# The opening of a fused recurrence and two expert layers: first maxima from the first chunk's own gates, and products that nobody reads

## The chip, the cores and the metric

The kernel runs on one core of a Trainium2 chip. A time is the device time of one execution in microseconds (us). The core has a matrix engine (TensorE, PE in the rows; its weight loads are PEld), a vector engine (DVE), a scalar engine (ACT), GpSimd (POOL) and the sync engine (SP), which here issues nearly all transfers between HBM and SBUF. Each engine takes its instructions strictly in the order written; between engines, semaphores hold an instruction until what it needs is there. Products land in PSUM, eight banks of 128 partitions x 512 floats.

## The reference, cut to what matters

Three layers follow one another: a gated linear recurrence over 768 steps (2 batches x 8 heads, head size 40), a gated MLP on the 1536 tokens (320 -> 1536 -> 320), and a mixture of 8 experts with the best two taken (320 -> 1024 -> 320). Everything is in float32. The change lies in the recurrence:

```python
m_new = max(f_t + m, i_t)              # running maximum, per batch and head
f_stab, i_stab = exp(f_t + m - m_new), exp(i_t - m_new)
C = f_stab * C + i_stab * outer(v_t, k_t)
n = f_stab * n + i_stab * k_t
y_t = sigmoid(o_t) * (C @ q_t) / max(|n @ q_t|, 1)
```

## The kernel before

The 768 steps are cut into 6 chunks of 128. A chunk of one batch (`ci` = 0 to 11; chunk `ci // 2`, batch `ci % 2`) is computed as attention inside the chunk plus a state `st[b]` carried from chunk to chunk. Let F be the sum of the forget gates since the chunk's start, a = i - F, and cm the running maximum of a. Then the weight of step s for step t is exp(a_s - Ml_t), where Ml = max(cm, what comes in from the chunks before). `g0` makes F, a and cm for all 96 (batch, head, chunk) rows (L418 to L420, 96 partitions x 128), `g1` and `g2` carry the maxima from chunk to chunk and make Ml (L429 to L439), which is also written to DRAM (`ml_d`), from where the later chunks read it spread over 128 partitions (`load_mb`, L378). The first two `ci` do not wait for that round trip: `gb` (L446, step `m`) spreads eight rows of Ml over 128 partitions by float32 products with a column of the identity matrix repeated 128 times, four heads to a PSUM bank of the tag `acc`, of which there are two.

The work of one `ci`, by the letters of the step table: `e` exponentials of the weights (ACT, four per half of the heads, L482); `s` products q.k (L500); `p` their multiplication with the weights (DVE L505) and the mask (POOL L506); `v` products with v (L557); `u` products k.v for the state (L518), `d` and `S` the state's decay and sum (L531, L539), `c`/`C` the state's part of the result (L526, L549); `y`, `z` division and gate (DVE L563 to L576); `t` transposes (L356); `X`, `x` the split of the result into two parts whose sum has float32 precision (ACT L340, DVE L343); `k` weighted keys (L490); `o` tanh of the output gate (L591).

The MLP's weight tiles go through a decode and split (`D` for the first, `N` for the second matrix, parts `r`, `a`, `b`, `c`, `h`/`H`, `l`; DVE L260, L263, L266, L298, L299, ACT L257, POOL L273). A unit of the MLP is `G` and `V` (eight products of 128x256 each, L363), `T` tanh, `U` the gating (DVE L884, L887), `H` and `L` a split, `J` the second matrix. Tokens of two `ci` make one unit's input.

Up to about 145 us the order is a table of words, `STEPS`, written out by hand; each engine gets its instructions in that order. After it, loops set the order. The words `w<n>g` and `w<n>a` issue n products of 128 weights by 512 columns in bfloat16 on a matrix of ones (`warm`, L734) into a PSUM bank of tag `gv` or `acc`; nothing reads them. `l` words issue loads: `lm`, `lq`, `lt` (maxima, q and k, tokens of a `ci`), `lu`, `ld` (weight tiles). SP issues transfers in that order and waits at each until the buffer is free. The tables of the experts, the routing and the last stage are not touched.

Of the kernel before, what the change touches and what calls it, by code (L numbers as in the profile page):

```python
# [53 lines left out]
o4 lu3 s4 e5.1 U0.2 w4g x3 G1.0 N0c V1.0 N0H lm6 p4.1 p4.0 u4 N0l T1.0 d4 H0.2 J0.0 G1.1 N1a C4 N1r N1b lu4 L0.2 ld2
K5 U1.0 H1.0 v4.0 o5 N1c e5.0 N1h T1.1 v4.1 S4 y4 lq6 lt6 s5 c5 D3a ld3 z4 D3b D3r C5 N1l w5g t4 X4 V1.1 p5.0 L1.0
lm7 U1.1 p5.1 D3c x4 J0.1 J0.2 e6.0 R0 e6.1 G1.2 V1.2 u5 d5 T1.2 U1.2 lq7 D3H H1.1 v5.0 v5.1 S5 D3l G1.3 lu5 y5 z5
N2r D4r s6 L1.1 p6.0 p6.1 V1.3 t5 T1.3 U1.3 N2a c6 K6 C6 X5 x5 J1.0 H1.3 lt7 lm8 lq8 K7 D4a N2b D4b D4c N2c v6.0
e7.0 lu6 L1.3 d6 G2.0 V2.0 T2.0 U2.0 H1.2 L1.2 v6.1 ld4 o6 y6 N2h D4h u6 S6 N2l e7.1 z6 H2.0 J1.1 L2.0 lt8 s7 p7.0
G2.1 V2.1 p7.1 c7 C7 o7 T2.1 U2.1 H2.1 t6 X6 J1.2 J1.3 D4l u7 L2.1 x6 G2.2 d7 v7.0 lm9 e8.0 T2.2 V2.2 U2.2 S7 lq9 R1
H2.2 e8.1 v7.1 s8 y7 z7 k8 G2.3 V2.3 T2.3 L2.2 p8.0 t7 c8 X7 U2.3 H2.3 o8 C8 p8.1 x7 d8 L2.3 J2.0 v8.0 u8 S8 e9.0  # L60
lt9 K9 e9.1 G3.0 V3.0 T3.0 U3.0 H3.0 v8.1 y8 L3.0 z8 G3.1 s9 p9.1 T3.1 p9.0 D5a c9 J2.1 C9 lm10 lq10 lt10 o9 V3.1
U3.1 e10.0 t8 D5b D5r X8 d9 D5c lm11 D5H G3.2 T3.2 J2.2 J2.3 x8 u9 v9.0 V3.2 H3.1 L3.1 D5l o10 U3.2 S9 v9.1 e10.1 y9
H3.2 z9 R2 lq11 s10 G3.3 p10.0 p10.1 J3.0 t9 V3.3 X9 N3r x9 T3.3 lu7 lt11 e11.0 U3.3 L3.2 H3.3 N3a c10 C10 G4.0 L3.3
# [1206 lines left out]
```

## Time and profile before

| | us |
|---|---|
| runs shown | 556.64, 552.83, 554.41 (median 554.41) |
| the profiled execution, first to last instruction | 551.0 |
| PE busy (weight loads) | 527.7 (506.0) |
| DVE, ACT, POOL busy | 342.6, 251.8, 202.4 |
| transfers | 73.14 MB, mean 133 GB/s |

The profiled execution has no whole time of its own in the page, only its span of 551.0 us; the median of the three runs is 3.4 us longer, and the runs differ by 3.8 us among themselves. A busy PE is not a PE at its peak: a product's end is modelled, and one that is stretched by a slow clock or by its weight load counts as busy all the same. PEclk is the clock that was granted, as a share of 2.4 GHz: 1.00 is 2.4 GHz and 0.50 is 1.2 GHz. Where the trace has no record of the clock yet, at the start of a kernel, the views print 1.00; what the clock was there is read from how long a product takes.

### The profile page before, as it was taken

To read this page: it belongs to the slowest core of one execution; us is meant where nothing else is said; L and a number is where in the kernel's file an instruction comes from. 1 tells how busy PE (TensorE), PEld (TensorE's weight loads), DVE (VectorE), ACT (ScalarE), POOL (GpSimd) and SP (SyncE) were. 2 spreads that over 40 slices of the span, in tenths; PEclk is the share of its full clock that TensorE was granted. 3 is DMA by queue.
4 is the path that set the end of the run, shared out by engine and by line. 5 is a ranking of instruction groups with operands and counts; after the bars stand their busy time and mean duration, and the time that the engine had idled before them with its cause. 6 is when DMAs were issued, how large, how long until landed. Compare 5 with 4: busy or idle time off the path is not lost.

```text
span 551.0 us, 10447 instructions
## 1 busy us (share of the span) xinstructions
PE 527.7 (96%) x3847; PEld 506.0 (92%) x3847; DVE 342.6 (62%) x914; ACT 251.8 (46%) x566; POOL 202.4 (37%) x375
## 2 busy tenths in 40 slices
PE   6999999999999999999999999799999999999993
PEld 4987999998999899999999999699999999999992
DVE  5469999798639988345448853982738283734420
ACT  3426555544345534355445733653646363543420
POOL 6323463332232332226556165214142414242322
PEclk9569999999999999999999999899999999999997
DMA  7839967441474644001112317564645464441403
GB/s 259 233 91 266 334 199 235 127 156 49 127 194 159 213 157 140 25 1 50 48 50 71 112 52 222 171 202 67 223 88 202 86 203 88 162 87 49 64 5 41
DMA packets 39908, 73.14 MB, mean 133 GB/s; under 512 B 3399, under 2 KB 25799, under 8 KB 39847
## 3 DMA queue, kind: packets, MB, share of 16 engines
q1 hardware_dynamic: 34807, 64.10, 36.1%
...
q14 instruction: 29, 0.24, 0.1%
...
## 4 chain that ended last, share of the span: by engine, by line
PE 79%; DVE 13%; ACT 2%; issue 2%; POOL 2%; DMA 1%; SPq 0%; POOLq 0%; ACTq 0%; DVEq 0%
PE gv L363 28%; PE acc L363 8%; PE ps_misc L557 3%; PE gv L1118 3%; PE gv L1119 3%; PE gv L1120 3%; PE acc L796 3%; PE acc L794 3%; PE acc L795 3%; PE ps_s L500 2%; PE ps_s L356 2%; PE acc L1120 2%; PE acc L1119 2%; PE acc L1118 2%; PE acc L1114 2%
## 5 line engine op out<-in xcount | busy, mean ns | idle before, releaser
L363 PE MATMUL gv<-x,wa 128*128 128x256 f32 (+3 forms) x1440 | 212.3, 295 | 4.9 <-ACT x L857 2.4
L363 PEld LDWEIGHTS gv<-x,wa 128*128 128x128 f32 x1440 | 194.8, 190 | 8.3 <-DVE ew L887 3.2
L893 POOL TENSOR_TENSOR h<-ew,h 128x256 fp32r<-128x256 f32 x72 | 57.2, 799 | 101.2 <-ACT h L890 66.4
L1136 POOL DMA_INDIRECT out_dram<-R,idi x33 | 49.5, 1501 | 61.4 <-ACT R L1131 43.3
L363 PE MATMUL acc<-x,wa 128*128 128x416 f32 (+2 forms) x288 | 58.3, 341 | 0.0
L884 DVE SCALAR_TENSOR_TENSOR ew<-ew,gv 128x256 f32<-128x256 f32 x72 | 30.0, 416 | 43.8 <-ACT ew L876 37.9
L876 ACT ACTIVATE ew<-gv 128x256 f32<-128x256 f32 x72 | 27.4, 382 | 63.6 <-PE gv L363 59.9
L332 DVE TENSOR_TENSOR wb<-draw,wb 128x640 fp32r<-128x640 f32 x32 | 27.6, 869 | 45.6 <-ACT wb L329 45.1
L1083 POOL CAST at<-at 128x32 fp32r<-128x32 f32 x72 | 21.5, 313 | 87.9 <-DVE at L1080 71.7
L890 ACT ACTIVATE h<-ew 128x256 fp32r<-128x256 f32 x72 | 29.8, 415 | 45.3 <-DVE ew L887 45.3
L363 PEld LDWEIGHTS acc<-x,wa 128*128 128x128 f32 x288 | 50.0, 189 | 0.4
L794 PE MATMUL acc<-wb,h 128*128 128x320 f32 x144 | 45.9, 320 | 0.0
L795 PE MATMUL acc<-wb,h 128*128 128x320 f32 x144 | 44.3, 309 | 0.0
L796 PE MATMUL acc<-wb,h 128*128 128x320 f32 x144 | 42.6, 313 | 0.4 <-POOL h L893 0.4
L1118 PE MATMUL gv<-wb,at 128*128 128x320 f32 x120 | 37.8, 315 | 0.0
L1120 PE MATMUL gv<-wb,at 128*128 128x320 f32 x120 | 37.2, 310 | 0.4 <-DVE at L1080 0.4
L1119 PE MATMUL gv<-wb,at 128*128 128x320 f32 x120 | 37.1, 309 | 0.0
L307 ACT ACTIVATE wa<-uraw 128x768 fp32r<-128x768 f32 x32 | 26.9, 840 | 12.9 <-DMA uraw<-in_w_dram 11.2
L506 POOL TENSOR_SCALAR_AFFINE_SELECT at<-at 128x512 f32<-128x512 f32 x24 | 17.4, 739 | 38.0 <-DVE at L505 28.8
L887 DVE SCALAR_TENSOR_TENSOR ew<-ew,gv 128x256 f32<-128x256 f32 x72 | 30.1, 417 | 1.7
L329 ACT ACTIVATE wb<-draw 128x640 fp32r<-128x640 f32 x32 | 23.2, 734 | 15.5 <-DMA draw<-in_w_dram 14.0
L298 DVE TENSOR_TENSOR wa<-uraw,wa 128x512 fp32r<-128x512 f32 x32 | 22.5, 703 | 9.7 <-ACT wa L307 9.4
...
## 6 DMA issues: line engine op xcount, KB each, us to landing
uraw<-in_w_dram SPq DMA_DIRECT2D x16, 768.0 KB, 4.8
...
uraw<-in_wup_dram SPq DMA_DIRECT2D x12, 768.0 KB, 9.0
...
```

The costliest lines, as they stand in the source:

```text
L363: m = PE.matmul(ps, w[:, k, ws], x[hl][:, t], start=n == 0, stop=n == len(seq) - 1)
L794: PE.matmul(o, hb[:, 0, os], w_[:, 0, q], start=j == 0, stop=False)
L795: PE.matmul(o, hb[:, 0, os], w_[:, 1, q], start=False, stop=False)
L796: PE.matmul(o, hb[:, 1, os], w_[:, 0, q], start=False, stop=j == len(tiles) - 1)
L884: m = V.scalar_tensor_tensor(t, t, 1.0, gv[:, 0], op0=OP.add, op1=OP.mult)
L887: V.scalar_tensor_tensor(t, t, 0.5, gv[:, 1], op0=OP.mult, op1=OP.mult)
L890: last["hi"] = A.activation(self.hb[:, 0], self.t, AF.Copy)
L893: P.tensor_tensor(self.hb[:, 1], self.t, self.hb.bitcast(F32)[:, 0], op=OP.subtract)
L1118: PE.matmul(acc[:m], h0, w[:, 0, f % 2], start=f == 0, stop=False)
L1119: PE.matmul(acc[:m], h0, w[:, 1, f % 2], start=False, stop=False)
L1120: PE.matmul(acc[:m], h1, w[:, 0, f % 2], start=False, stop=f == EJ - 1)
L1136: s = P.indirect_dma_start(out=out, out_offset=bass.IndirectOffsetOnAxis(ap=ID[v][:m, j:j + 1], axis=0), in_=y, in_offset=None, compute_op ...
```

## The change

Five things are changed together.

1. A new input `first` (80 x 2 x 128, 82 KB) holds the gates of chunk 0 three times, on partitions 0 to 15, 32 to 47 and 64 to 79. `i0` and `i1` make F, a and cm of chunk 0 alone from it, before `g0`. For chunk 0 nothing comes in from before, so its Ml is its cm.
2. cm is cut into three bfloat16 pieces whose sum is cm, one on each of the three partition groups, and `gb` spreads a row by one bfloat16 product with a 0/1 matrix `sel` that adds the three pieces (80 rows, 128 columns).
3. The `w` words of the opening are new in number, place and PSUM tag (`m` is `ps_misc`, `s` is `ps_s`), and one `w4g` further on is gone.
4. The state update is one `scalar_tensor_tensor` per pair of heads, four in all, in place of a multiplication and an addition on all four pairs; the words `d` are gone.
5. The first steps stand in another order, and so do the first transfers: both `ci`'s q, k and tokens come before the two weight tiles, and the two decodes of the weights stand later.

```diff
-g0 o0 w9g D0a D0b s0.02 g1 g2 lm2 lq2 s0.1357 D0r o1 m0.0 e0.0 D0c D0H s0.46 m1.0 e1.0 s1 ld0 p0.0 p1.0 la3 lt2 g3
-m0.1 e0.1 D1a m1.1 e1.1 v0.0 p0.1 w1a v1.0 lb3 w3a v0.1 D0l p1.1 v1.1 D1b y0 e2.0 g4 lu2 D1r z0 lm3 y1 z1 t0 X0 s2
-x0 D1c D1H t1 w4a X1 x1 g5 k0 D1l k1 e2.1 p2.1 p2.0 G0.0 V0.0 G0.1 T0.1 u1 V0.1 lt3 T0.0 u0 S1 U0.0 H0.0 L0.0 D2a S0
+w11g i0 w2g i1 w2g m0.0 m0.1 s0 e0.0 g0 w4g e0.1 m1.0 p0.0 w4g g1 m1.1 w3g g2 p0.1 e1.0 e1.1 s1 p1.0 v0.0 w4s o0 o1 p1.1
+v0.1 y0 D0a D0b w4s v1.0 D0r D0c D0H lm2 lq2 ld0 v1.1 w3s z0 t0 w4s lq3 lt2 X0 g3 x0 y1 z1 t1 w2s D0l X1 x1 g4 lu2 lm3 D1a D1b e2.0 D1r s2 D1c D1H g5 k0
+D1l k1 e2.1 p2.1 p2.0 G0.0 V0.0 G0.1 T0.1 u1 V0.1 lt3 T0.0 u0 S1 U0.0 H0.0 L0.0 D2a S0
...
+    N0 = 80
+    fst = wk.tile([N0, 6, 2, L], F32, name="x", bufs=X_BUFS).rearrange("p a b l -> p (a b) l")
+    SP.dma_start(fst[:, 0:2], first)
+    F0, a0, cm0, r0 = (fst[:, i] for i in range(2, 6))
+    pieces, mid = (fst[:, 6].bitcast(BF)[:, i * L:(i + 1) * L] for i in range(2))
+    sel = fst[:, 7].bitcast(BF)[:, 0:B * H]
...
+    for i in range(0, N0, 32):
+        r = slice(i, min(i + 32, N0))
+        V.tensor_scalar(sel[r], diff[r, i:i + B * H], 0.0, None, op0=OP.is_equal)
...
-    load_qk(0)
-    up_load(0)
-    load_qk(1)
     for ci in range(2):
         MB[ci] = at_tile([128, H, L])
     for ci in range(2):
-        TK[ci] = at_tile([128, 2 * DM + 328])
-    load_tk_in(0)
-    load_tk_in(1)
+        load_qk(ci)
+        load_tk(ci)
+    up_load(0)
     up_load(1)
...
+    def i0():
+        V.tensor_tensor_scan(F0, fst[:, 1], pre[0:N0, 4:4 + L], 0.0, op0=OP.add, op1=OP.add)
+        V.tensor_tensor(a0, fst[:, 0], F0, op=OP.subtract)
+        t = ps_misc()
+        PE.transpose(t[:, 0:N0], a0, ident[:N0, :N0])
+        A.activation(cols[:, 0, :, :, 0], t[:, 0:B * H].rearrange("p (b h) -> p b h", b=B), AF.Copy)
+    def i1():
+        V.tensor_tensor_scan(cm0, a0, a0, -1e30, op0=OP.max, op1=OP.max)
+        V.tensor_copy(pieces, cm0)
+        V.tensor_tensor(r0, cm0, pieces, op=OP.subtract)
+        V.tensor_copy(pieces[32:64], r0[32:64])
+        V.tensor_copy(mid[64:N0], r0[64:N0])
+        V.tensor_tensor(pieces[64:N0], r0[64:N0], mid[64:N0], op=OP.subtract)
...
-            r = (ci * H + 2 * i + half) * NC
-            PE.matmul(m[:, i], ident[:G96, r:r + 1].to_broadcast([G96, 128]), Ml, start=True, stop=True)
+            r = ci * H + 2 * i + half
+            PE.matmul(m[:, i], sel[:, r:r + 1].to_broadcast([N0, 128]), pieces, start=True, stop=True)
...
-        def p_d():
-            if 0 < c < NC - 1:
-                V.tensor_tensor(st[b], st[b], dec2[:, b, :, c:c + 1].to_broadcast([104, 4, 82]), op=OP.mult)
...
-                V.tensor_tensor(st[b], st[b], u, op=OP.add)
+                for q in range(4):
+                    V.scalar_tensor_tensor(st[b][:, q], st[b][:, q], dec2[:, b, q, c:c + 1], u[:, q], op0=OP.mult, op1=OP.add)
...
-            warm(n, {"g": "gv", "a": "acc"}[st_])
+            warm(n, {"g": "gv", "a": "acc", "m": "ps_misc", "s": "ps_s"}[st_])
```

How the instructions stand, at three places. First, TensorE from the first instruction on, before (`ones` is the matrix of the unread products, L734; L446 spreads the maxima; runs of the same product stand once, with "..." for the rest):

```order
L422 MATMUL ps_misc<-shift,x 1x96
L423 MATMUL ps_misc<-shift,x 1x96
L424 MATMUL ps_misc<-ident,x 128x96
L734 LDWEIGHTS ones
L734 MATMUL gv<-ones 128x512
...
L500 MATMUL ps_s<-at 128x128 x2
L433 MATMUL ps_misc<-one_87,rows 96x1
L500 MATMUL ps_s<-at 128x128 x4
L446 MATMUL acc<-x,ident 128x128 x4
```

and the same stretch of the change (L752 is now the unread product, L426 the transpose of `i0`, L467 the spreading, L521 the q.k products, L443 to L445 `g0`):

```order
L752 LDWEIGHTS ones
L752 MATMUL gv<-ones 128x512
...
L426 MATMUL ps_misc<-ident,x 128x80
...
L467 LDWEIGHTS x
L467 MATMUL acc<-x 128x128
...
L521 MATMUL ps_s<-at 128x128 x8
L443 MATMUL ps_misc<-shift,x 1x96
L444 MATMUL ps_misc<-shift,x 1x96
L445 MATMUL ps_misc<-ident,x 128x96
```

Before, TensorE's first instruction needs cm of all 96 rows. Now eleven unread products stand first, then the transpose, four more unread products and the eight spreading products of `ci` 0, and `g0` comes behind the q.k products. In all 43 unread products stand ahead of the first unit of the MLP, where there were 17.

Second, the vector engine around the second token tile's split (the second L343 of the piece before, the second L351 of the one after; L260, L263, L266 or L268, L271, L274 are the decode steps a, b, c of a weight tile, L298 and L299 or L306 and L307 its last step), before:

```order
L343 TENSOR_TENSOR x<-ps_misc,x 128x3x128
L266 ISA dec<-uraw,dec 128x1536
L343 TENSOR_TENSOR x<-ps_misc,x 128x3x128
L459 COPY cols<-acc 128x288
L490 TENSOR_TENSOR kw_112<-at,cols 128x8x40
L298 TENSOR_TENSOR wa<-dec,wa 128x512
L299 TENSOR_TENSOR wa<-dec,wa 64x256
L490 TENSOR_TENSOR kw_113<-at,cols 128x8x40
L505 SCALAR_TENSOR_TENSOR at<-at,ps_s 128x4x128 x2
L884 SCALAR_TENSOR_TENSOR ew<-ew,gv 128x256
```

and in the change:

```order
L306 TENSOR_TENSOR wa<-dec,wa 128x512
L307 TENSOR_TENSOR wa<-dec,wa 64x256
L351 TENSOR_TENSOR x<-ps_misc,x 128x3x128
L268 TENSOR_SCALAR dec<-uraw 128x768
L271 SCALAR_TENSOR_TENSOR dec<-uraw,dec 128x768
L274 ISA dec<-uraw,dec 128x1536
L480 COPY cols<-acc 128x288
L511 TENSOR_TENSOR kw_117<-at,cols 128x8x40
L306 TENSOR_TENSOR wa<-dec,wa 128x512
L307 TENSOR_TENSOR wa<-dec,wa 64x256
L511 TENSOR_TENSOR kw_118<-at,cols 128x8x40
```

The last step of the first weight tile now stands just ahead of the split, and all three decode steps of the second tile behind it; before, they lay ahead of it. Behind the second L511 the two orders are the same but for the state update.

Third, SP's first transfers, before:

```order
L168 DMA y<-in_gates_dram 96x256
L388 DMA at<-in_qk_dram 104x1024
L232 DMA uraw<-in_wup_dram 128x1536
L388 DMA at<-in_qk_dram 104x1024
L395 DMA at<-in_tok_dram 128x968 x2
L232 DMA uraw<-in_wup_dram 128x1536
L438 DMA ml_d<-x 96x128
```

and in the change:

```order
L168 DMA x<-in_first_dram 80x256
L173 DMA y<-in_gates_dram 96x256
L396 DMA at<-in_qk_dram 104x1024
L403 DMA at<-in_tok_dram 128x968
L240 DMA uraw<-in_wup_dram 128x1536 x2
L459 DMA ml_d<-x 96x128
```

The gates of chunk 0 lead, and the weight tiles `uraw` are last of the first group; the pair L396, L403 stands twice.

## Rows read from the trace of the kernel before

**Rows 1.** The page: the span from first to last instruction.

```profile
span 551.0 us, 10447 instructions
```

**Rows 2.** Stretches: length, busy time (instructions) of five engines, PEclk, DMA share, GB/s.

```profile
9.57:12.98 3.41, 3.41 (x26) 2.94 (x25) 1.89 (x5) 2.06 (x5) 1.00 (x11) 1.00 0.95 382
12.98:36.88 23.90, 23.90 (x119) 20.99 (x118) 12.12 (x26) 8.85 (x28) 6.83 (x11) 0.50 0.64 185
40.00:94.00 54.00, 52.41 (x461) 48.44 (x460) 51.43 (x105) 30.45 (x81) 25.14 (x42) 1.00 0.80 255
354.32:357.73 3.41, 3.22 (x11) 3.08 (x12) 2.68 (x18) 1.58 (x4) 1.34 (x1) 0.50 0.81 223
```

**Rows 3.** The chain of waits to 40 us: start, length, engine, tile, line, records.

```profile
0.92 0.17 DVE ones L176
...
4.17 0.48 PE ps_misc L422 x2
...
5.32 3.84 PE gv L734 x9
...
13.14 2.00 PE acc L446 x8
...
25.69 3.27 PE ps_misc L557 x16
...
30.59 2.01 PE ps_s L500 x16
...
35.35 3.57 PE gv L363 x24
```

**Rows 4.** The same view from 45 to 66 us.

```profile
47.94 1.29 PE gv L734 x6
...
55.43 0.44 PE ps_misc L356 x4
...
56.72 1.09 PE ps_s L500 x16
...
63.25 1.71 PE ps_misc L557 x16
```

**Rows 5.** Timeline: start, length, engine, line, what; in brackets the idle time before.

```profile
12.59 1.14 ACT L482 ACTIVATE at<-acc,cols 128x128 f32<-128x128 f32 x4 [0.20 <-PE acc L446]
```

**Rows 6.** Timeline of the vector engine, 3 to 41 us.

```profile
3.69 0.42 DVE L420 TENSOR_TENSOR_SCAN x<-x 96x128 f32<-96x128 f32 x1
...
17.25 0.69 DVE L505 SCALAR_TENSOR_TENSOR at<-at,gv 128x512 f32<-128x512 f32 x1 [2.80 <-PE gv L500]
...
29.19 0.17 DVE L572 SCALAR_TENSOR_TENSOR den<-ps_misc,den 128x8 f32<-128x8 f32 x1
...
29.90 0.49 DVE L576 TENSOR_TENSOR y<-at,den 128x320 f32<-128x320 f32 x1
...
31.63 0.95 DVE L266 CUSTOM_DVE_ANT_0 dec<-uraw,dec 128x1536 uint16<-128x1536 uint16 x1
34.21 0.56 DVE L343 TENSOR_TENSOR x<-ps_misc,x 128x384 fp32r<-128x384 f32 x1 [1.63 <-ACT x L340]
...
35.57 0.71 DVE L298 TENSOR_TENSOR wa<-dec,wa 128x512 fp32r<-128x512 f32 x1
36.31 0.42 DVE L299 TENSOR_TENSOR wa<-dec,wa 64x256 fp32r<-64x256 f32 x1
36.76 0.49 DVE L490 TENSOR_TENSOR kw<-at,cols 128x320 f32<-128x320 f32 x1
...
39.65 0.42 DVE L884 SCALAR_TENSOR_TENSOR ew<-ew,gv 128x256 f32<-128x256 f32 x1 [1.20 <-PE ps_misc L518]
```

**Rows 7.** Transfers issued from 17 to 19 us: count, KB each, us to landing.

```profile
uraw<-in_wup_dram SPq DMA_DIRECT2D x1, 768.0 KB, 12.8
```

**Rows 8.** The two lines of the state update: durations in ns, min/median/max.

```profile
L531 DVE TENSOR_TENSOR st<-st,dec x8: 487/662/1041, 49.0 to 115.4; 104x328 f32<-104x328 f32 x8
L539 DVE TENSOR_TENSOR st<-st,ps_misc x8: 487/489/496, 49.6 to 120.3; 104x328 f32<-104x328 f32 x8
```

More of the change, by code (lines that the diff above doesn't have):

```diff
@@ L54 @@
[L54 to L63, printed above, removed]
@@ new lines @@
+v0.1 y0 D0a D0b w4s v1.0 D0r D0c D0H lm2 lq2 ld0 v1.1 w3s z0 t0 w4s lq3 lt2 X0 g3 x0 y1 z1 t1 w2s D0l X1 x1 g4 lu2 lm3 D1a D1b e2.0 D1r s2 D1c D1H g5 k0
+D1l k1 e2.1 p2.1 p2.0 G0.0 V0.0 G0.1 T0.1 u1 V0.1 lt3 T0.0 u0 S1 U0.0 H0.0 L0.0 D2a S0 lm4 D2r U0.1 v2.0 s3 c2 D2b
+e3.0 D2c C2 H0.1 D2h k2 v2.1 w2a y2 o2 z2 u2 p3.0 lq4 lt4 e3.1 p3.1 t2 w6g X2 x2 S2 c3 C3 D2l L0.1 v3.0 K3 v3.1 y3 o3
+z3 lm5 G0.2 e4.1 u3 S3 K4 e4.0 w1g T0.2 lq5 V0.2 N0a N0r N0b t3 X3 ld1 lt5 c4 o4 lu3 s4 e5.1 U0.2 x3 G1.0 N0c V1.0 N0H
@@ new lines @@
+lm6 p4.1 p4.0 u4 N0l T1.0 H0.2 J0.0 G1.1 N1a C4 N1r N1b lu4 L0.2 ld2 K5 U1.0 H1.0 v4.0 o5 N1c e5.0 N1h T1.1 v4.1 S4 y4
+lq6 lt6 s5 c5 D3a ld3 z4 D3b D3r C5 N1l w5g t4 X4 V1.1 p5.0 L1.0 lm7 U1.1 p5.1 D3c x4 J0.1 J0.2 e6.0 R0 e6.1 G1.2 V1.2
+u5 T1.2 U1.2 lq7 D3H H1.1 v5.0 v5.1 S5 D3l G1.3 lu5 y5 z5 N2r D4r s6 L1.1 p6.0 p6.1 V1.3 t5 T1.3 U1.3 N2a c6 K6 C6 X5
+x5 J1.0 H1.3 lt7 lm8 lq8 K7 D4a N2b D4b D4c N2c v6.0 e7.0 lu6 L1.3 G2.0 V2.0 T2.0 U2.0 H1.2 L1.2 v6.1 ld4 o6 y6 N2h
+D4h u6 S6 N2l e7.1 z6 H2.0 J1.1 L2.0 lt8 s7 p7.0 G2.1 V2.1 p7.1 c7 C7 o7 T2.1 U2.1 H2.1 t6 X6 J1.2 J1.3 D4l u7 L2.1 x6
@@ new lines @@
+G2.2 v7.0 lm9 e8.0 T2.2 V2.2 U2.2 S7 lq9 R1 H2.2 e8.1 v7.1 s8 y7 z7 k8 G2.3 V2.3 T2.3 L2.2 p8.0 t7 c8 X7 U2.3 H2.3 o8
+C8 p8.1 x7 L2.3 J2.0 v8.0 u8 S8 e9.0 lt9 K9 e9.1 G3.0 V3.0 T3.0 U3.0 H3.0 v8.1 y8 L3.0 z8 G3.1 s9 p9.1 T3.1 p9.0 D5a
+c9 J2.1 C9 lm10 lq10 lt10 o9 V3.1 U3.1 e10.0 t8 D5b D5r X8 D5c lm11 D5H G3.2 T3.2 J2.2 J2.3 x8 u9 v9.0 V3.2 H3.1 L3.1
+D5l o10 U3.2 S9 v9.1 e10.1 y9 H3.2 z9 R2 lq11 s10 G3.3 p10.0 p10.1 J3.0 t9 V3.3 X9 N3r x9 T3.3 lu7 lt11 e11.0 U3.3
+L3.2 H3.3 N3a c10 C10 G4.0 L3.3 N3b v10.0 N3c v10.1 s11 T4.0 e11.1 V4.0 U4.0 ld5 G4.1 T4.1 p11.0 H4.0 y10 z10 L4.0 o11
@@ L68 @@
+J3.1 N3H c11 C11 V4.1 U4.1 H4.1 t10 X10 N3l x10 J3.2 G4.2 T4.2 p11.1 v11.0 V4.2 v11.1 D6r D6a G4.3 J3.3 R3 U4.2 H4.2
+L4.1 T4.3 y11 z11 D6b D6c L4.2 lu8 t11 J4.0 V4.3 X11 x11 G5.0 V5.0 D6H D6l T5.0 U4.3 H4.3 U5.0 J4.1 J4.2 G5.1 L4.3
+V5.1 T5.1 H5.0 L5.0 U5.1 H5.1 L5.1 G5.2 V5.2 J4.3 R4 T5.2 G5.3 V5.3 T5.3 U5.2 H5.2 L5.2 U5.3 H5.3 L5.3 J5.0
 """
@@ L134, in tile_mlstm_glu_moe @@
 @with_exitstack
-def tile_mlstm_glu_moe(ctx: ExitStack, tc: tile.TileContext, gates, qk, tok, wup, wdn, w1, w2, wgn, noise, out):
+def tile_mlstm_glu_moe(ctx: ExitStack, tc: tile.TileContext, first, gates, qk, tok, wup, wdn, w1, w2, wgn, noise, out):
     nc = tc.nc
@@ L424, in g0 @@
         PE.transpose(Q["a"][:, 256:352], a, ident[:G96, :G96])
-        A.activation(cols[:, 0].rearrange("p b h c -> p (b h c)"), Q["a"][:, 256:352], AF.Copy)
+        A.activation(cols[:, 0, :, :, 1:], Q["a"][:, 256:352].rearrange("p (b h c) -> p b h c", b=B, h=H)[:, :, :, 1:], AF.Copy)
     def g1():
@@ L909, in act @@
             (g0, g1, g2, g3, g4, g5)[n]()
+        elif what == "i":
+            (i0, i1)[n]()
         elif what == "w":
-            warm(n, {"g": "gv", "a": "acc"}[st_])
+            warm(n, {"g": "gv", "a": "acc", "m": "ps_misc", "s": "ps_s"}[st_])
         elif what == "m":
@@ L939, in act @@
             else:
-                f[{"y": "y", "z": "y2", "t": "t", "o": "o", "u": "u", "S": "st", "c": "c", "C": "cg", "d": "d"}[what]]()
+                f[{"y": "y", "z": "y2", "t": "t", "o": "o", "u": "u", "S": "st", "c": "c", "C": "cg"}[what]]()
     for word in STEPS.split():
@@ L1215, in prep @@
     a = {}
+    r = np.stack([i["i_gate"][:, :, :L].reshape(B * H, L), i["f_gate"][:, :, :L].reshape(B * H, L)], 1)
+    a["first"] = np.zeros((80, 2, L), f)
+    for o in (0, 32, 64):
+        a["first"][o:o + B * H] = r
     a["gates"] = np.stack([i["i_gate"].reshape(G96, L), i["f_gate"].reshape(G96, L)], 1)
@@ L1250, in prep @@
     return {n: v.view(np.int64) if n in ("wup", "wdn") else v for n, v in a.items()}
-_INS = ["gates", "qk", "tok", "wup", "wdn", "w1", "w2", "wgn", "noise"]
+_INS = ["first", "gates", "qk", "tok", "wup", "wdn", "w1", "w2", "wgn", "noise"]
 def kernel(**inputs):
```

8 lines of the change are left out of this document (1 added, 7 removed).

## The prediction

> **What bounds the kernel now.** I read the granted clock of stretches first, since the page's busy shares are alike nearly everywhere. TensorE's clock stood at 1.2 GHz (0.50) from 12.98 to 36.88 us and at 2.4 GHz for the 3.41 us before that [rows 2]. Up to 9.57 us no record exists, but the products tell: nine unread ones took 3.84 us there, 0.427 each, and six took 1.29 us, 0.215 each, at 47.94 us, where the clock is 2.4 GHz [rows 3, 4]. So the clock rose once, right behind those nine products, and fell again under the float32 products of q.k and of the maxima; it rose for good only behind four unread products and the first products of the MLP. The chain of waits comes next: from 4.17 us to the end of the 24 products at 38.92 us it never leaves TensorE [rows 3]. So in the opening TensorE is the bound, mostly at half speed, and it idles for the first 4.17 us. Then I read the busy table on from 40 us: the vector engine is busy 51.43 of 54 us until 94 us and transfers have 0.80 of their engines [rows 2]. What the opening gains must get past these two. Behind 145 us nothing is changed.
>
> **TensorE's sum in the opening, now.** The first unread product needs only the matrix of ones, written by 1.09 us [rows 3], so TensorE starts at 1.2 instead of 4.17. Up to the first unit (24 products, at 35.35 before):
> - 43 unread products: 15 stand ahead of the first spreading product, and I take these at 0.427 = 6.4; 28 at 0.215 = 6.0.
> - q.k for three `ci`, 1.09 each at 2.4 GHz (2.01 before) = 3.3 [rows 3, 4].
> - products with v for two, 1.71 for 16 records (3.27 before), so 3.4 for both [rows 3, 4].
> - transposes of two tiles, 0.44 each = 0.9 [rows 4].
> - the twelve short float32 passes of `g0`, `g1`, `g4` and `i0`: 0.24 each at half speed, from 0.48 for two [rows 3], so 1.5 at full.
> - 16 bfloat16 spreading products of 128 columns. The trace has none. Below: a quarter of a 512-column product, 0.054; above: the float32 pass it replaces, 0.25 at half speed (2.00 for eight), so 0.125. I take 0.1, since the weights are loaded anew each time: 1.6 (0.9 to 2.0).
>
> Together 23.1, so TensorE could reach the first unit at 24.3, 11 us sooner. Whether the others let it is the next sum.
>
> **The chain through ACT and the vector engine.** Chunk 0's three scan steps take at most 0.42 each and run at the place of the old ones, which ended at 4.1 [rows 6]; three tiny `sel` writes ahead and five small steps of the pieces behind (each under 0.42) put the pieces at 5.6 to 6.5. TensorE gets to the spreading only at 8.0 (1.2 + 6.4 + a transpose), so this is covered. From there:
> 1. Exponentials: four groups at 1.14 [rows 5]. Between the first and the second, ACT copies the columns from `g0`, which stands behind q.k on TensorE: 8.2 to 9.4, then 10.4 to 13.9.
> 2. The last two weight multiplications, 0.69 each [rows 6], and q.k of `ci` 1, which ends near 14: done at 15.5.
> 3. Decode a, b, c of tile 0, at most 0.95 each [rows 6], some 2.5: 18.0. Its transfer now comes last but one of a first group of 3.6 MB; at the 382 GB/s of [rows 2] that is 9.4 us, over by 12, so it is there.
> 4. Division and gate of `ci` 0: 1.4 (0.17 more than the stretch from 29.19 to 30.39 [rows 6]): 19.5. TensorE still has products with v and three unread ones until 20.0; transpose 20.5.
> 5. The two halves of the split, under 0.56 each [rows 6]: 21.7. `ci` 1's division 23.2, transpose 23.7, the last step of tile 0 (1.13) beside it, split: 24.9, against 34.77 before.
> 6. TensorE: two unread products, `g4`, q.k of `ci` 2: first unit at 25.7, against 35.35, 9.7 us sooner.
>
> **What moved behind it.** Tile 1's decode a, b, c (2.5) lay under TensorE's wait before and now stands after the split; then two steps near 0.49 and the last step, 0.71 + 0.42 [rows 6]. That ends at 24.9 + 2.5 + 1.0 + 1.2 = 29.6, where it ended at 36.73. The second unit's gate needs it: eight products of some 0.95 end at 30.6 instead of 38.92. So of the 9.7 us 1.5 is given back and 8.2 is left, and the vector engine's first gating comes at about 31.5 instead of 39.65 [rows 6]. POOL's copy of the tile runs beside the two steps; what sticks out is under 0.5, in the upper end.
>
> **The state update.** Eight pairs of 0.66 (median) and 0.49 [rows 8] = 9.2 us go; 32 instructions of 82 columns with PSUM come. None is in the trace: 0.17 at 8 columns and 0.42 at 256 [rows 6] bound it, 5.4 to 13.4 in all; by columns it is 0.24, 7.8. I take nothing either way (-1.4 by the interpolation, less the gaps). The Trainium skill, page "VectorE: DVE Perf Modes", section "Rules for kernel authors", speaks against this step: chained vector instructions are not to be fused for speed, their count is to be kept small. Here the count doubles; at the 0.16 that the 8-column row leaves as fixed part, 16 more would cost 2.6 us by the rule alone, but the eight multiplications over 328 columns that go give the same back.
>
> The dropped `w4g` is 0.86 us of TensorE [rows 4], where other work fills in: nothing, at best 0.9.
>
> **Sum.** 8.2, less 0.7 for the decode work that now falls into a stretch where the vector engine has only 2.6 us idle [rows 2]: **7.5 us**. The profiled span of 551.0 [rows 1] becomes 543.5; the median of the runs is 554.41, 3.4 above it, and I let that stay: **547 us**.
>
> **Rivals.**
>
> *Once more at half (549.5).* The clock falls back inside the opening, as it did at 12.98 us although TensorE counted as busy, and as at 354.32 us, where it stood low for 3.41 us [rows 2]. Half speed for 3.41 us costs 1.7; twice that 3.4. Gain 4 to 6. For it: the float32 products during which it fell are still there. Against: unread products now stand between nearly all of them. The Trainium skill, page "TensorE: Matmul & The Clock Gate", Part 1, says that the ramp costs less than 1% of a typical kernel's span, which would cap the gain at 5.5 us and put the time at 549 or more; in this trace 23.9 us at half speed on the bounding engine are over 4% of the span [rows 2], so I let the rows decide.
>
> *The loads become last (550).* The third weight tile was issued near 17.6 and took 12.8 us [rows 7], so it was there at 30.4; its decode stands right behind the gating that began at 39.65. Now its issue still waits for decode c of tile 0 (18.0), so it lands near 31, and its decode is due at 32. A spare of 9 us shrinks to 1, and two more loads of 0.5 MB follow at once, 4 us at 255 GB/s [rows 2]. If they mix, the vector engine, which takes its instructions in order, waits up to 3 or 4 us there: gain 4 to 5. Against it: no transfer stands in the chain of waits up to 40 us now [rows 3], and a spare of 1 us is still a spare.
>
> *The clock doesn't hold, and the products are dead weight (558.5).* At 1.2 GHz throughout, TensorE's sum is 43 x 0.427 = 18.4, q.k 6.0, v 6.5, transposes 1.8, short passes 2.9, spreading 1.7 to 4.0: 37.3 to 39.6, first unit at 38.5 to 40.8 instead of 35.35, 3.2 to 5.5 later. It decides if TensorE gets less than about a quarter of this work done at 2.4 GHz. For it: 17 unread products, spread out, did not hold the clock before. Against: nine in a row raised it, and here fifteen stand in a row at the start. This is also the case in which the change doesn't do what it says.
>
> **How the numbers follow.** 7.5 us holds (gain 6 to 9): 0.54. Once more at half: 0.16. Loads last: 0.20. Clock not held: 0.10. A measurement of this kernel can tell about 1% from no change, 5.5 us, so faster means under 548.9. That takes nine tenths of the first case, a third of the second and a quarter of the third: 0.59, with a little off for the spread of the runs: 0.58. Slower means above 560, the far end of the last case: 0.04. Same: 0.38. The range leaves out the last case and half a tenth at either end: 543.5 (TensorE's own 11 us) to 552.5.
>
> **What would show it.** Right: unread products at 0.215 from some 9 us on, 2.4 GHz in most of 10 to 30 us, the first unit near 26, the first gating near 31.5, and the rows behind it shifted by the same 7 to 8 us at 94 and 145 us. Wrong: a long 0.50 between 10 and 30 us; the vector engine waiting for a transfer at the third tile's decode; the shift shrinking between 32 and 94 us, with the vector engine without idle time; more than 1.2 us per state update.

## The result, and the profile after

The changed kernel takes 546.9 us (median of four runs, 545.98 to 549.06), the kernel before on the same chip 553.93 (four runs, 552.83 to 556.64): ratio 0.9875, 95% interval 0.9849 to 0.9900. The profiled span is 544.2 us, 6.8 less than before [rows 1]. Forecast were 547.0, and 543.5 for the span.

In the changed kernel L752 is an unread product, L467 a spreading product, L521 q.k, L575 a product with v, L364 a transpose, L371 a product of the MLP, L503 the exponentials, L268, L271, L274 and L306, L307 the decode and split of a weight tile (`a`, `b`, `c` and the last step), L351 the split of x, L557 the fused update, L902 the gating.

The page first: its span, and TensorE's clock in 40 slices.

```profile
span 544.2 us, 10489 instructions
...
PEclk9999999999999999999999999899999999999997
```

Then the stretches, columns as in [rows 2]: the first three cover the opening from the clock's rise on, the fourth is the one of before from 40 to 94 us, 9 us earlier.

```profile
4.93:9.57 4.64, 4.51 (x41) 2.88 (x40) 3.63 (x13) 1.91 (x8) 3.02 (x30) 1.00 1.04 249
9.57:12.98 3.41, 3.41 (x33) 2.09 (x31) 1.64 (x6) 3.17 (x13) 1.79 (x15) 1.00 1.00 379
12.98:30.00 17.02, 14.24 (x113) 11.29 (x110) 14.36 (x29) 6.51 (x18) 4.39 (x7) 1.00 0.85 262
31.00:85.00 54.00, 52.45 (x457) 48.11 (x455) 51.45 (x115) 30.81 (x82) 26.16 (x43) 1.00 0.81 252
```

The clock was granted at 2.4 GHz from 4.93 us and did not fall until 346.26; before it was at 1.2 GHz from 12.98 to 36.88 [rows 2]. From 31 us on the vector engine is as full as it was, 51.45 of 54 us against 51.43.

The chain of waits through the opening, columns as in [rows 3]:

```profile
3.98 0.43 DVE x L423
...
6.28 0.29 DVE x L436
6.61 0.61 PE acc L467 x8
7.22 1.09 PE ps_s L521 x16
...
16.06 0.86 PE ps_s L752 x4
16.93 1.71 PE ps_misc L575 x16
18.64 0.65 PE ps_s L752 x3
...
24.03 0.48 DVE dec L268
24.54 0.97 DVE dec L271
25.63 0.96 DVE dec L274
...
27.75 0.72 DVE wa L306
28.51 0.98 PE gv L371 x6
```

Up to 6.57 us the vector engine is the bound (the chain names POOL before 3.98, but the vector engine's own writes fill that time, see the timeline below), then TensorE without a gap to 19.7. Then the split, `ci` 1's division and the second tile's decode follow, nearly all on the vector engine. The first unit's products start at 24.76 us, wait from 26.93 on for the second tile, and end at 29.48. A q.k of 16 records takes 1.09 where it took 2.01, the products with v 1.71 where they took 3.27 [rows 3]. The vector engine's timeline, columns as in [rows 6]:

```profile
1.62 2.19 DVE L197 TENSOR_SCALAR x<-hn 32x16 bf16<-32x16 f32 x3
3.98 0.42 DVE L423 TENSOR_TENSOR_SCAN x<-x,pre 80x128 f32<-80x128 f32 x1
...
23.48 0.56 DVE L351 TENSOR_TENSOR x<-ps_misc,x 128x384 fp32r<-128x384 f32 x1 [0.29 <-ACT x L348]
...
28.48 0.42 DVE L307 TENSOR_TENSOR wa<-dec,wa 64x256 fp32r<-64x256 f32 x1
...
30.54 0.41 DVE L902 SCALAR_TENSOR_TENSOR ew<-ew,gv 128x256 f32<-128x256 f32 x1
31.33 0.64 DVE L268 TENSOR_SCALAR dec<-uraw 128x768 int32<-128x768 int32 x1
```

The first gating begins at 30.54, where it began at 39.65 [rows 6]: 9.1 us sooner. The third tile's decode (31.33) follows with no idle time in brackets, so its load was there.

**Where the 9.1 us went.** The 72 gatings (L884 before, L902 now) are landmarks that both kernels pass in the same order. The 37th begins at 189.05 instead of 198.02 (9.0 sooner), the 72nd at 300.22 instead of 308.03 (7.8), the last expert's output rows at 534.39 instead of 541.49 (7.1). So the opening's gain holds to 200 us and 1.2 us is lost between 200 and 300 us, in code that the change doesn't touch. The 37th and the 72nd on the vector engine's timelines, before and then changed:

```profile
198.02 0.41 DVE L884 SCALAR_TENSOR_TENSOR ew<-ew,gv 128x256 f32<-128x256 f32 x1
...
308.03 0.42 DVE L884 SCALAR_TENSOR_TENSOR ew<-ew,gv 128x256 f32<-128x256 f32 x1 [1.24 <-ACT ew L876]
```

```profile
189.05 0.41 DVE L902 SCALAR_TENSOR_TENSOR ew<-ew,gv 128x256 f32<-128x256 f32 x1
...
300.22 0.42 DVE L902 SCALAR_TENSOR_TENSOR ew<-ew,gv 128x256 f32<-128x256 f32 x1 [1.29 <-ACT ew L894]
```

### The profile page after: what moved, and what is told of

Its sections match the earlier page's. It is cut to its first block, busy times and chain, and to the rows that moved or that the text cites. A ratio compares the mean times of both kernels' runs of the same rounds, so it can differ in the third digit from the quotient of the medians.

```text
span 544.2 us, 10489 instructions
## 1 busy us (share of the span) xinstructions
PE 521.6 (96%) x3854; PEld 497.1 (91%) x3854; DVE 344.2 (63%) x941; ACT 250.9 (46%) x567; POOL 200.1 (37%) x375
## 4 chain that ended last, share of the span: by engine, by line
PE 75%; DVE 12%; DMA 3%; POOL 3%; issue 3%; ACT 2%; SPq 0%; POOLq 0%; DVEq 0%; ACTq 0%
PE gv L371 28%; PE acc L371 7%; PE ps_misc L575 3%; PE acc L814 3%; PE acc L812 3%; PE acc L813 3%; PE gv L1138 3%; PE gv L1140 3%; PE gv L1139 3%; DMA uraw<-in_w_dram 2%; PE ps_s L521 2%; PE ps_s L364 2%; PE ps_misc L547 2%; POOL xs L711 2%; PE acc L1138 2%
## 5 line engine op out<-in xcount | busy, mean ns | idle before, releaser
L371 PE MATMUL gv<-x,wa 128*128 128x256 f32 (+3 forms) x1440 | 215.0, 297 | 6.4 <-ACT x L875 2.4
L371 PEld LDWEIGHTS gv<-x,wa 128*128 128x128 f32 x1440 | 196.0, 190 | 10.8 <-DVE ew L905 2.6
L371 PE MATMUL acc<-x,wa 128*128 128x416 f32 (+2 forms) x288 | 58.4, 341 | 0.0
L902 DVE SCALAR_TENSOR_TENSOR ew<-ew,gv 128x256 f32<-128x256 f32 x72 | 30.0, 417 | 44.3 <-ACT ew L894 37.6
L1103 POOL CAST at<-at 128x32 fp32r<-128x32 f32 x72 | 20.2, 282 | 91.0 <-DVE at L1100 70.9
L371 PEld LDWEIGHTS acc<-x,wa 128*128 128x128 f32 x288 | 50.0, 189 | 0.4
L306 DVE TENSOR_TENSOR wa<-uraw,wa 128x512 fp32r<-128x512 f32 x32 | 22.0, 686 | 9.7 <-ACT wa L315 9.4
L527 POOL TENSOR_SCALAR_AFFINE_SELECT at<-at 128x512 f32<-128x512 f32 x24 | 16.3, 695 | 31.4 <-DVE at L526 22.4
## 6 DMA issues: line engine op xcount, KB each, us to landing
uraw<-in_wup_dram SPq DMA_DIRECT2D x12, 768.0 KB, 10.1
```

The costliest lines, as they stand in the source:

```text
L371: m = PE.matmul(ps, w[:, k, ws], x[hl][:, t], start=n == 0, stop=n == len(seq) - 1)
L902: m = V.scalar_tensor_tensor(t, t, 1.0, gv[:, 0], op0=OP.add, op1=OP.mult)
```

## The experiments

The main theory: the gain is a TensorE list run at 2.4 GHz instead of 1.2, and the unread products hold that clock. The rivals: it is the new way to the maxima, the new order or the fused update. The last three columns are starts in the one profiled execution of each kernel, in us. Each ratio is against the kernel before on the same chip; the chips differ from row to row, so medians of different rows compare only roughly.

| kernel | median | ratio (95% interval) | 1.2 GHz in the opening | 1st gating | 37th | 72nd |
|---|---|---|---|---|---|---|
| before | 553.93 | 1 | to 9.57, 12.98 to 36.88 | 39.65 | 198.02 | 308.03 |
| changed | 546.90 | 0.9875 (0.9849 to 0.9900) | to 4.93 | 30.54 | 189.05 | 300.22 |
| e1 no products | 548.98 | 0.9905 (0.9874 to 0.9937) | to 33.77 | 35.04 | 193.59 | 304.75 |
| e2 leading only | 547.34 | 0.9865 (0.9806 to 0.9924) | to 4.48, 11.31 to 31.79 | 32.73 | 191.32 | 302.48 |
| e3 before, products | 553.53 | 0.9958 (0.9928 to 0.9988) | to 6.71, 10.12 to 20.36, 30.60 to 37.42 | 40.24 | 198.33 | 308.40 |
| e4 old update | 546.44 | 0.9860 (0.9812 to 0.9907) | to 4.47 | 30.53 | 188.75 | 299.92 |
| e5 float32 spreading | 549.66 | 0.9896 (0.9837 to 0.9955) | see there | | | |
| e6 old addresses | 543.17 | 0.9794 (0.9749 to 0.9839) | to 5.54 | 30.56 | 188.58 | 298.65 |
| e7 before, moved | 554.96 | 1.0015 (0.9985 to 1.0045) | to 10.02, 13.44 to 37.33 | 39.91 | 198.48 | 309.65 |
| e8 half the products | 544.98 | 0.9823 (0.9785 to 0.9860) | to 6.38, 20.04 to 30.28 | 31.66 | 189.87 | 299.88 |
| e9 decode ahead | 543.80 | 0.9810 (0.9774 to 0.9847) | to 6.49 | 30.82 | 188.88 | 298.89 |
| e10 best order | 542.09 | 0.9777 (0.9739 to 0.9815) | to 6.15 | 29.16 | 186.89 | 296.96 |
| e11 x at 128 | 544.01 | 0.9793 (0.9760 to 0.9825) | to 5.23 | 28.85 | 186.61 | 297.71 |
| e12 memsets later | 543.34 | 0.9807 (0.9779 to 0.9835) | to 6.58 | 29.20 | 186.85 | 296.94 |

### e1: no unread products

```diff
-w11g i0 w2g i1 w2g m0.0 m0.1 s0 e0.0 g0 w4g e0.1 ...
+i0 i1 m0.0 m0.1 s0 e0.0 g0 e0.1 ...
```

> The changed kernel without the 43 unread products of the opening; all else, scans, pieces and order included, is kept. Theory (the gain is TensorE's clock, and the products hold it): the clock is at 0.50 from the first record until the products of the MLP have run for a few us; q.k 2.0 us instead of 1.09, products with v 3.3 instead of 1.7; first unit near 29 instead of 26.6 and its products at 0.21 instead of 0.12; first gating 34 to 37 us instead of 31.3; time 549.5 to 552. Rival 1 (the gain is the new way to the first maxima and the new order; TensorE is not the bound any more): 546 to 547.5, first gating within 1 us. Rival 2 (all of the gain hangs on the products): 554.

The main theory's mechanism holds. The chain of waits of e1:

```profile
6.61 1.01 PE acc L467 x8
7.62 2.01 PE ps_s L521 x16
...
14.95 6.98 PE ps_misc L575 x32
...
27.22 2.01 PE ps_s L521 x16
29.23 5.08 PE gv L371 x24
```

All of it is at half speed, and the first gating comes 4.5 us later than in the changed kernel. But it is still 4.6 us sooner than in before, so half of the gain is left without these products. Where that half comes from is argued, not tested alone. In before TensorE never pauses from 4.17 us to the first unit [rows 3], and in e1 it starts no sooner (4.78) and at no higher clock, so its list must have become shorter: before, 17 unread products (8.0 us busy) and 32 records of float32 spreading (7.0 us) stood in it; in e1 there are none of the first, and 16 bfloat16 spreading products with 2.3 us. The spreading, in the busy table of before and of e1:

```profile
L446 PE MATMUL acc<-x,ident 96*128 96x128 f32 x32 | 7.0, 398 | 0.0
```

```profile
L467 PE MATMUL acc<-x 80*128 80x128 bf16 x16 | 2.3, 309 | 1.4 <-DVE x L436 1.4
```

How much of it is the spreading, how much the unread products of before, and what the new order lets through, no run separates. The whole time (548.98 against 546.90) shows 2.1 of the 4.5 us, with intervals that overlap, and lies 0.5 us under the theory's range; the trace separates the two kernels.

### e2: only the leading fifteen

```diff
 w11g i0 w2g i1 w2g m0.0 m0.1 s0 e0.0 g0
-w4g e0.1 m1.0 p0.0 w4g g1 m1.1 w3g g2 ...
+e0.1 m1.0 p0.0 g1 m1.1 g2 ...
```

> The changed kernel with only the 15 leading unread products (ahead of the first spreading product); the 28 that stand between the float32 products are left out. Theory (holding the clock needs them): 2.4 GHz from about 5 us, back at 1.2 GHz within 10 us under q.k and the products with v, up again with the MLP; first unit 27 to 29, time 548 to 550.5. Rival (once up, the clock stays up through float32 products alone): 0.99 or 1.00 from 5 us on, first unit 26 to 26.6, time 546 to 547.

The theory held: TensorE's clock stood at 1.00 up to 11.31 us, then at 0.50 to 31.79, with TensorE counted as busy for 17.91 of 20.48 us:

```profile
4.48:11.31 6.83, 5.47 (x57) 3.82 (x57) 5.20 (x19) 3.66 (x15) 4.47 (x44) 1.00 1.03 319
11.31:31.79 20.48, 17.91 (x96) 16.83 (x93) 15.44 (x30) 7.23 (x20) 5.70 (x12) 0.50 0.80 256
```

Of the 4.5 us, 2.3 are the rise (35.04 to 32.73) and 2.2 the holding (32.73 to 30.54), each less what the products themselves cost. The mean granted clock of the other three executions is 0.975, of the traced one 0.972, and of the changed kernel's four 0.991 to 0.993, so the clock fell in all of e2's. The time (547.34) is 0.7 us under the theory's range.

### e8: half of the later products

```diff
-e0.0 g0 w4g e0.1 m1.0 p0.0 w4g g1 m1.1 w3g g2 ... v0.0 w4s o0 ...
+e0.0 g0 w2g e0.1 m1.0 p0.0 w2g g1 m1.1 w2g g2 ... v0.0 w2s o0 ...
```

> The kernel with the old addresses (e6) and about half of the unread products behind the leading 15: 14 instead of 28. Theory (TensorE is the path from 6.8 to 19.3 us, and the later products are a price paid there): the clock still holds; 3.0 us of products go from that stretch, the next limits (weight multiplications, products with v) let 1 to 2.5 us of it through; first gating 28 to 29.5 us against 30.56; time 541 to 542.5 where e6 had 543.2. Rival (14 are too few): the clock falls back for some us between 10 and 30 us, first gating 31 to 33 us, time 544 to 546.

The rival was right. The clock fell at 20.04 us and the first gating came at 31.66, 1.1 us after e6's. Fourteen did not hold it, neither here nor, by the mean granted clock, in the others: 0.980 to 0.988 in the six executions, where e6's six have 0.991 to 0.994.

```profile
6.38:20.04 13.66, 12.09 (x108) 8.96 (x106) 9.57 (x23) 6.90 (x24) 6.47 (x38) 1.00 0.77 255
20.04:30.28 10.24, 8.60 (x45) 7.94 (x46) 9.13 (x19) 3.80 (x11) 2.10 (x4) 0.50 1.02 313
```

### e3: the kernel before with unread products

```diff
-g0 o0 w9g D0a D0b s0.02 ... o1 m0.0 e0.0 D0c D0H s0.46 m1.0 e1.0 s1 ld0
+w9g g0 o0 w4g D0a D0b s0.02 ... o1 w4g m0.0 e0.0 D0c D0H s0.46 w4g m1.0 e1.0 w4g s1 ld0
```

> The kernel before with unread products alone: its nine now stand ahead of the first scan's transposes instead of behind them, and four each stand at four places between the float32 products (25 in all); scans, spreading and order are those of before. Theory (in before TensorE is the bound from 4.2 to 38.9 us, so a held clock must pay there too): products run from 1.2 us, the clock is at 2.4 GHz from about 5 us through most of the opening, first gating 32 to 35 us instead of 39.65; time 549 to 552. Rival 1 (the float32 products of the maxima let the clock fall all the same): 0.50 from some 13 us on, the 16 added products are paid, first gating 39 to 42 us, time 553.5 to 556. Rival 2 (the old order makes ACT and the vector engine the next bound): clock held, but first gating 36 to 38 us, time 551 to 553.

In the profiled execution (554.38 us) rival 1 is right. The clock rose at 6.71 us, three sooner than before, and fell at 10.12:

```profile
10.12:20.36 10.24, 10.24 (x39) 7.66 (x39) 2.23 (x5) 2.82 (x7) 2.29 (x12) 0.50 0.72 232
20.36:30.60 10.24, 9.05 (x80) 7.86 (x79) 6.40 (x15) 5.83 (x19) 3.21 (x3) 1.00 0.78 253
30.60:37.42 6.82, 6.82 (x36) 5.17 (x35) 4.84 (x11) 2.15 (x6) 1.94 (x3) 0.50 0.26 80
```

In this execution the products did not pay for themselves: the first gating is 0.6 us later than before. The ten runs spread from 548.62 to 559.04, the widest here, with a ratio of 0.9958, and they follow their mean granted clock. The five executions at 0.982 to 0.988 took 548.62 to 552.69 us, all of them less than the shortest of before's seventeen (553.16); the five at 0.974 to 0.979, the profiled one among them, took 554.38 to 559.04. So unread products alone can pay in the old order too, by 6.5 us against before's median (555.13) in the best execution, but there they don't hold the clock reliably, and in the median they gain little.

### e5: float32 spreading

```diff
-PE.matmul(m[:, i], sel[:, r:r + 1].to_broadcast([N0, 128]), pieces, ...)
+PE.matmul(m[:, i], ident[:B * H, r:r + 1].to_broadcast([B * H, 128]), cm0[:B * H], ...)
```

> The changed kernel with the maxima spread from the float32 row in one float32 product each; the five steps that make bfloat16 pieces are left out. Theory (the pieces buy little): the 16 products take 0.125 us each instead of 0.055, 1.1 us more on TensorE, while the vector engine is ready 1.3 us sooner; first gating 30.3 to 31.5 us against 30.5, time 546.5 to 548. Rival (the pieces are needed to hold the clock, since float32 products let it fall): 0.50 appears between 8 and 25 us, first gating 33 us or later, time 549 to 551.

By the time (549.66, ratio 0.9896) it is nearer to the rival, but the interval reaches the changed kernel's ratio. The profiled execution took 557.19 us, 7.5 more than the median, so its starts are left out of the table; in it the clock fell at 9.83 us, rose, and fell again from 16.66 to 33.73, with a mean of 0.976. One other execution is like it (558.14 us, 0.975). The three that took 548.64 to 549.66 us have 0.991 or 0.992, as the changed kernel has, so no such fall is in them. They have no trace, and a clock that rises late leaves the same mean (e1: 0.992). Whether bfloat16 pieces are needed to hold the clock is not settled, and what costs those three some 2.8 us is open.

### e4: the old state update

```diff
-for q in range(4):
-    V.scalar_tensor_tensor(st[b][:, q], st[b][:, q], dec2[:, b, q, c:c + 1], u[:, q], op0=OP.mult, op1=OP.add)
+V.tensor_tensor(st[b], st[b], u, op=OP.add)      # and, as the step d, the multiplication of before
```

> The changed kernel with the state update of before: one multiplication ahead and one addition behind, at their old places, instead of four fused instructions. Theory (the fused update is a small gain): first gating unchanged at 30.5 us; the vector engine works 8 times 0.2 us more, 0.92 us becoming 0.61 and 0.50, so the shift against before at 113 us is 0 to 1.5 us smaller than the 9.0 of the changed kernel; time 547 to 548.5. Rival (the rule against fusing is right here): the shift is larger by 0.5 to 2 us, time 545 to 546.5.

My theory fell. With the old update the 37th gating is 0.3 us sooner (188.75 against 189.05), with the same first gating. The whole times (546.44 and 546.90) can't tell the two apart, but the stretch from the first to the 37th gating can: 158.47 to 158.59 us in the four traces with the fused update and the change's addresses (changed, e1, e2, e5), 158.22 in e4. Four fused instructions take 0.92 us, the old pair 0.61 and 0.50; the vector engine's timelines of the changed kernel and of e4:

```profile
39.80 0.92 DVE L557 SCALAR_TENSOR_TENSOR st<-st,dec,ps_misc 104x82 f32<-104x82 f32 x4
```

```profile
39.79 0.61 DVE L544 TENSOR_TENSOR st<-st,dec 104x328 f32<-104x328 f32 x1
40.43 0.50 DVE L560 TENSOR_TENSOR st<-st,ps_misc 104x328 f32<-104x328 f32 x1
```

By busy time the fused form is 0.2 us shorter, and still it loses. A reason that fits, argued only: the multiplication can run before the product k.v is there, the fused form cannot, so 0.92 instead of 0.50 us stand behind that product. The Trainium skill, page "VectorE: DVE Perf Modes", section "Rules for kernel authors", advises against fusing for speed; the sign agrees, at 0.3 us in the trace.

### e7 and e6: where the tiles lie

The changed kernel claims a tile under the name `x` first in its pool. That moves the six split x tiles, the inputs of the MLP's products, from address 158304 to 120352 of each partition, and the attention tiles behind them. e7 does that alone to the kernel before; e6 undoes it in the changed one.

```diff
 # e7, in the kernel before
+    gt = wk.tile([G96, 6, L], F32, name="x", bufs=X_BUFS)
     G = wk.tile([G96, 2, L], F32, name="y")
 # e6, in the changed kernel
+    G = wk.tile([G96, 2, L], F32, name="y")
+    diff = wk.tile([128, 128], F32, name="hn")
+    MB = {ci: wk.tile([128, H, L], F32, name="at", bufs=AT_BUFS) for ci in range(2)}
     fst = wk.tile([N0, 6, 2, L], F32, name="x", bufs=X_BUFS)
```

> The kernel before with one line moved: the buffer of the gates, which has the name of the split x tiles, is claimed first in its pool, so that the split x tiles lie at the address they have in the changed kernel (120352 instead of 158304) and the attention tiles at 162400 instead of 125536. No instruction changes. Theory (the later loss of about 2 us in the changed kernel comes from where the tiles lie): products of the first MLP start 0.120 us apart instead of 0.118, time 1.5 to 2.5 us above before, ratio 1.003 to 1.0045. Rival (the 2 ns are of the single run or of the changed order): 0.118 as before, ratio 1.000 within 0.001.

> The changed kernel with its tiles claimed in the old order, so that split x and attention tiles lie at the addresses of the kernel before. No instruction changes. Theory (placement): products of the first MLP 0.118 us apart instead of 0.120, the shift against before stays at 9 us to the end instead of shrinking to 7.1; time 544.5 to 545.5. Rival (the 2 ns have another cause): 0.120, time 546.5 to 547.5.

The 16 products of a unit's two halves, from the chains of waits of before, e7, the changed kernel and e6, in this order:

```profile
255.95 1.88 PE gv L363 x16
```

```profile
257.08 1.92 PE gv L364 x16
```

```profile
253.48 1.91 PE gv L371 x16
```

```profile
255.10 1.89 PE gv L373 x16
```

So a product starts 0.118 us after the one ahead of it at the old address, and 0.120 at the new one, in both programs. Between the 37th and the 72nd gating before needs 110.01 us and e6 110.07; e7 needs 111.17 and the changed kernel 111.17: 1.1 us more, in both. The placement theory holds in the traces; e7's whole time (1.4 us over before) doesn't reach outside its interval. e6 is 3.7 us under the changed kernel, its ratio's interval below that of the change. That is more than the theory said and more than the address shows: 0.5 us up to the 37th gating and 1.1 between the 37th and the 72nd.

### e11: 32 bytes further

```diff
+    mcol = wk.tile([G96, 2], F32, name="mcol", bufs=1)
     fst = wk.tile([N0, 6, 2, L], F32, name="x", bufs=X_BUFS)
```

> e10 with one small tile claimed ahead of the split x tiles, so that these, and the row tile behind them, lie 32 bytes further on (158336, a multiple of 128, instead of 158304); nothing else moves. Theory (the 2 ns of a product in the first MLP hang on how the address of x lies against some power of two): products 0.113 to 0.116 us apart instead of 0.118, shift growing by 1 to 4 us between 200 and 308 us, time 1.5 to 5 us under e10. Rival 1 (it is the distance or order of the regions, not alignment): 0.118, same time as e10 within 0.5 us. Rival 2: 0.120, 1.5 to 2.5 us above e10.

Rival 2: the slow spacing is back with 32 bytes, from e10 with all else equal.

```profile
250.97 1.93 PE gv L374 x16
253.78 1.91 PE gv L374 x16
```

The 37th to the 72nd gating take 111.10 us against e10's 110.07. Nothing else moves but the row tile behind x and the small tile itself, so a new region is not needed as a cause; 32 bytes of start address are enough. By which rule, three addresses (158304 good, 120352 and 158336 not) can't say.

### e9 and e10: the second tile's decode ahead

```diff
-v1.1 w3s z0 t0 w4s lq3 lt2 X0 g3 x0 ... lm3 D1a D1b e2.0 D1r s2
+v1.1 w3s z0 D1a D1b t0 w4s lq3 lt2 X0 g3 x0 ... lm3 e2.0 D1r s2          # e9
+v1.1 w3s z0 D1a D1b t0 w4s lq3 lt2 X0 g3 D1r x0 ... lm3 e2.0 s2          # e10, and the old update
```

> The kernel with the old addresses (e6) and two steps of the second tile's decode (0.55 and 0.96 us of the vector engine) moved ahead, into its wait from 18.9 to 20.3 us for the first split. Theory (behind 19 us the vector engine sets when the first two units run, since the second tile's decode stands behind the split): first unit 1.0 to 1.4 us sooner, first gating 29.2 to 29.6 us against 30.56, and the shift keeps it; time 541.8 to 542.3. Rival 1 (ACT or TensorE is as late): less than 0.4 us. Rival 2 (the gain is lost behind 40 us, where the vector engine has no idle time): first gating 29.4, shift at 113 us back at 9.2, time 543.2.

> The kernel with the old addresses (e6), the state update of before (e4), and the decode of the second tile ahead as in e9, now with its ACT step ahead of the third chunk's exponentials too: in e9 the vector engine's last decode step waited for that ACT step until 25.9 us. Theory: last step of tile 1 ends at 27.2 to 27.8 us instead of 28.9, first gating 29.0 to 29.6 us against 30.56 (up to 0.5 later if the clock rises late), shift at 113 us 10.3 to 11.0 us and held to 308 us; time 541 to 542. Rival (TensorE or ACT is as late as the vector engine): first gating 30.2 to 30.8, time 542.5 to 543.5.

e9 gained nothing, as its first rival said: the last decode step waited for its ACT step, which stood behind the third chunk's exponentials. The chain of e9:

```profile
23.82 1.27 ACT at L503 x4
25.09 0.80 ACT uraw L267
25.91 0.96 DVE dec L276
```

With that step ahead too, e10's first gating comes at 29.16, the first unit's 24 products go through without a wait, and TensorE is the bound there:

```profile
24.05 1.09 PE ps_s L521 x16
25.14 3.02 PE gv L373 x24
```

e10 has the lowest median of all, 542.09 (ratio 0.9777), and its 72nd gating is 11.1 us sooner than before's. Against e6 the times overlap; the trace gives 1.4 us at the first gating and 1.7 at the 72nd, the latter with the old update's 0.3 in it.

### e12: memsets behind the pieces

```diff
-w11g i0 w2g i1 w2g m0.0
+w9g i0 w1g i1 w1g m0.0
...
-    for i in range(2):            # ahead of the opening
-        P.memset(kw[i], 0.0)      # now at the end of i1
```

> e10 with POOL's two large memsets (0.52 us each) behind the pieces of the maxima instead of beside the three tiny sel writes, and 11 instead of 15 leading unread products, so that TensorE is free when the pieces are. Theory (POOL's work beside them makes the vector engine's 16-column writes take 1.35, 0.62 and 0.19 us): each takes about 0.2 us, the first scan starts near 2.8 instead of 3.98, pieces are ready near 5.4 instead of 6.56, spreading starts near 6.0 instead of 6.9 and first gating comes at 28.2 to 28.7 us instead of 29.16; time 541 to 542. Rival 1 (the writes are long by themselves, or the other POOL work is as bad): first scan still past 3.6, gain under 0.3 us. Rival 2 (four products fewer keep the clock low for longer, or a transfer is not there yet): spreading earlier, but first gating at 29 us or later.

The edit did not do what it was for: POOL still ran the two memsets ahead of the pieces, at 2.59 and 3.26. They ended 0.8 us later than in e10, and so did the first of the three 16-column writes, which took 2.18 us (the other two 0.16 and 0.17). The first scan began at 4.33, and the first gating came at 29.20 against e10's 29.16. What happens without memsets beside the writes is not tested.

```profile
1.62 2.54 DVE L199 TENSOR_SCALAR x<-hn 32x16 bf16<-32x16 f32 x3
2.59 0.51 POOL L436 MEMSET kw<- 128x512 f32 x1
3.26 0.51 POOL L436 MEMSET kw<- 128x512 f32 x1
```

## Why the prediction came out as it did

The forecast was right in sign and size, and the likeliest case is the one that happened: TensorE's list runs at 2.4 GHz and the opening gains. That the total is within 0.4 us at the last rows is in part luck: the opening gained 0.9 us more than forecast and the decode work cost 0.6 less, against 1.9 us behind the 37th gating that the forecast had at nothing.

- **The clock** was the cause named, and e1, e2 and e8 show it for 4.5 of the 9.1 us at the first gating. The 4.6 us that e1 still gains without the unread products the prediction did not set apart; its sum has only the new spreading, at 1.6 us (1.4 us busy in the trace). What failed is a detail of it: I took all fifteen leading products at 0.427 us, so spreading at 8.0; the clock rose at 4.93, and it began at 6.61.
- **The first writes** were not covered by the leading products: I gave the three `sel` writes tiny times, they took 2.19 us together and held the first scan to 3.98. Pieces were ready at 6.56, at the late end of the forecast (5.6 to 6.5), and they, not TensorE, set the start of the spreading. The trace of before had a warning: a write of 9 columns took 1.36 us there, and it too ended just behind POOL's two memsets (3.05 and 3.01):

```profile
1.69 1.36 DVE L198 CAST ebase<-y 128x9 bf16<-128x9 f32 x1
```

- **The chain through the vector engine** came out 0.7 to 1.0 us early all along: first split 20.84 (forecast 21.7), second 24.04 (24.9), last step of the second tile 28.9 (29.6), first gating 30.54 (31.5). The gain there is 9.1 instead of 8.2.
- **The second tile's decode moved behind** was rightly seen as what gives part of it back. I put that at 1.5 us; e10 gets 1.4 of it by moving the decode and its ACT step back ahead.
- **The state update** I took at nothing; it costs 0.3 us (e4), although its busy time fell as the interpolation said, from 1.11 to 0.92 us where it is shown.
- **The decode work in the full stretch** I took at 0.7; the shift at the 37th gating is 9.0 against 9.1 at the first, so 0.1, with the update's 0.3 and the address's 0.5 (e6) in it. No loss by the decode work is to be seen.
- **What was missing** is the address of the x tiles: 1.2 us between the 37th and the 72nd gating (e6, e7). No view of the kernel before could show it, but the diff did show that a tile of the name `x` is claimed first. A last 0.7 us goes between there and the end, where e6 gains 0.7 (10.1 us sooner at the last rows, 541.49 against 531.41). From the 72nd gating to the last of the indirect output transfers the traces take 233.6 us (e6) to 236.3 (e11), in no order of the addresses (e1 234.2 at the change's, e10 234.6 at the old ones), so 0.7 us there may well be the scatter of single executions; its cause is open.
- **The sum:** 9.1 less 0.1, 1.2 and 0.7 is 7.1 at the last rows, 6.8 in the span; forecast 7.5.
- **The rivals:** no 0.50 appears up to 346 us (against "once more at half" and "not held"), and the third tile's decode waits for no load (against "loads last"). The case of the dead weight did occur where it was not expected: in the profiled execution of e3. The Trainium skill, page "TensorE: Matmul & The Clock Gate", Part 1, puts the cost of the ramp under 1% of a typical span; the part that hangs on the products here, 4.5 us at the first gating, is 0.8% of 551.0, so it agrees. My rival took that as a cap on the whole gain, and half of the gain has another source (e1).
